# Sixteen more one-column matmuls at the head of TensorE's program, and half the columns on zeros behind the first scores, in a fused attention and feed-forward kernel

## The chip, the core and the metric

The kernel runs on one core of a Trainium2 chip. The core has four engines that compute: TensorE (PE for its matmuls, PEld for the loads of their stationary operands), VectorE (DVE), ScalarE (ACT) and GpSimd (POOL). SyncE (SP) issues the transfers, which sixteen DMA engines carry out. The metric is device time in microseconds, lower is better.

## What is computed

```python
# q, k, v: (8, 8, 576, 64); w_in (512, 2048), w_out (2048, 512)
scores = q @ k.T / sqrt(64)
# heads 0..3: local mask, 0 <= i - j < 32; heads 4..7: strided mask, i >= j and i % 32 == j % 32
attn = softmax(where(mask, scores, -1e9))
x = (attn @ v) laid out as (4608 tokens, 512 channels)
out = gelu(x @ w_in) @ w_out
```

## The kernel before, in words

The 4608 tokens are cut into 9 tiles of 512. Each tile goes through 16 pieces of the hidden layer: `ffn_h` sums a [128 x 512] block in 12 matmuls (lines 758 to 760: every operand is split into a rounded part and a rest, so each product takes three matmuls), `ffn_g` applies GELU on ScalarE and splits the result, and `ffn_o` adds the block's contribution to the output in another 12 matmuls (lines 796 to 798). The attention that feeds tile t + 1 is worked out beside the hidden layer of tile t: local heads with small matmuls on TensorE and a softmax on VectorE and ScalarE, strided heads almost wholly on VectorE.

The first tile has nothing to hide behind. Its local blocks are four jobs, L0 to L3 (`local_job`): scores by 8 matmuls of the program from the block's `qk` load (line 322), four masked score reductions on VectorE (line 280), four exponentials on ScalarE (line 285), sum and reciprocal (289, 292), a scaling (298, on VectorE for L0, L2 and L3), four transposes on TensorE (line 328), a copy (330), 8 matmuls with v (line 336), and the split of the result (305, 307). Its strided heads are two halves, `a0` and `b0` (`half_tile`: scores at line 455, mask and softmax at 464 to 478, transposes at 482, copy of the transposed weights into `va` at 484), which `strided_tile` (`A0`) joins: 32 matmuls of [32 x 32] per half at line 498 and transposes on VectorE at 503. The copy at 484 of the second half stands in the program behind the matmuls of the first half, and it reads a PSUM tile into which these matmuls write too.

The order of all this is written out by hand in the string `START`. Each word advances one job by a step (`L2` is the next step of block 2, `a0` the next of the first strided half), or issues a load: `q2 q0 q1 q3` are the loads of the four blocks' queries and keys (line 222), `S0` and `T0` those of the strided queries and keys (423), `v0` to `v3` the values (229), `w0`, `W0`, `w1` and on the weights (153), `B0` the strided values (441), `K1` the keys of the second tile (237). While the string is run, the order on all five engines is the string's. A word `z` and a digit is filler: one matmul on zeros into a spare PSUM tile (line 949), with 512 columns shifted right by the digit, so `z0` has 512, `z1` 256 and `z2` 128. In the main loop behind the string TensorE, VectorE and ScalarE stay in the order of the program; SyncE and GpSimd are ordered there by the framework's scheduler, which estimates when things happen.

Ahead of the string TensorE's program has a lead-in on zeros: one-column matmuls (line 897) and one matmul with 512 columns (line 898). A matmul with 32-bit floating-point operands is issued as two in the trace: the 48 of line 897 stand there as 96, each with its own load of weights; the small matmuls of the attention and the filler are doubled likewise. Those of the hidden layer, in another format, are not.

Of the kernel before, what the change touches and what calls it, by code (L numbers as in the profile page):

```python
# [47 lines left out]

NB = 16
START = """  # L50
    q2 q0 L2 z1 L0 L2 q1 S0 L0 L2 T0 L1 L2 L2 q3 L2 L1 v1 L2 L0 L0 v0 L1 v2 L0 L2 a0 w0 L0 a0 L1 a0 a0 b0 L3
    a0 b0 L1 b0 a0 b0 B0 L1 L3 b0 z0 L0 w1 L2 L3 b0 W0 a0 v3 a0 w2 b0 a0 b0 b0 K1 c0 L3 L2 L1 z2 a0 w3 L3 z2
    b0 L1 a0 L3 c0 z2 A0 W1 b0 A0 c1 c0 w6 w4 L2 c0 L0 L3 A0 L0 w5 L1 c1 A0 L1 w8 L3 A0 z0 c0 d0 e L0 L0 L3
    L3 L1 L3 w7 h0 E c1 f0 d0 w9 s1 c2 c2 d0 c1 f0 d0 c1 f1 c2 d0 V1 L4 f0 c3 d1 L5 d1 w10 f0 c3 w11 c2 c2
# [32 lines left out]
def attn_ffn_kernel(ctx: ExitStack, tc: tile.TileContext, qk, vl, qka, va, qs, ks, vs, s1, w, out):  # L87
# [732 lines left out]
    for u in range(U0, NU + 1):  # L820
# [12 lines left out]
        if av and qk_:  # L833
# [14 lines left out]
            i = next(i for i, x in enumerate(av) if x[1] == 0.6)  # L848
# [42 lines left out]
    def nil(p, n):  # L891
        return nc.const_aps.tensor(0.0, [p, n], F32)

    lead_in = ps_h.tile([P, TT], F32, name="lead_in", tag="H")
    for i in range(48):
        h = i % HL
        nc.tensor.matmul(lead_in[h * 32:h * 32 + 1, 0:1], nil(D, 1), nil(D, 1), start=True, stop=True, tile_position=(0, h * 32))
    nc.tensor.matmul(lead_in, nil(P, P), nil(P, TT), start=True, stop=True)
# [320 lines left out]
```

## Time and profile before

| what | value |
|---|---|
| three runs | 846.58, 848.91 and 2593.85 us |
| median | 848.91 us |
| profiled execution, own time | 848.29 us |
| its span, first to last instruction | 846.5 us (1.8 us lie outside it) |
| mean granted TensorE clock over the span | 0.996 of full speed |

Times in the views are microseconds from the start of the span. A row of the timeline has start, length, engine, line, operation, output and input with their shapes, and how many instructions were merged; in brackets the time for which the engine stood idle before them and what ended that, "issue" being a wait that nothing in the trace explains. A releaser is the event that came last before the wait ended, and can be another engine's that happened to finish then. Matmuls overlap, so the step from one start to the next is what one costs, and the length is more.

### The profile page before, as it was taken

To read this page: it belongs to the slowest core of one execution; us is meant where nothing else is said; L and a number is where in the kernel's file an instruction comes from. 1 tells how busy PE (TensorE), PEld (TensorE's weight loads), DVE (VectorE), ACT (ScalarE), POOL (GpSimd) and SP (SyncE) were. 2 spreads that over 40 slices of the span, in tenths; PEclk is the share of its full clock that TensorE was granted. 3 is DMA by queue.
4 is the path that set the end of the run, shared out by engine and by line. 5 is a ranking of instruction groups with operands and counts; after the bars stand their busy time and mean duration, and the time that the engine had idled before them with its cause. 6 is when DMAs were issued, how large, how long until landed. Compare 5 with 4: busy or idle time off the path is not lost.

```text
span 846.5 us, 15032 instructions
## 1 busy us (share of the span) xinstructions
PE 838.3 (99%) x5442; PEld 690.0 (82%) x5442; DVE 640.3 (76%) x1859; ACT 441.0 (52%) x862; POOL 18.1 (2%) x88
## 2 busy tenths in 40 slices
PE   8999999999999999999999999999999999999997
PEld 5788888888888888888888888888888888888886
DVE  6899989995999589958999698878887988521110
ACT  6898866552664355544553266545552456332222
POOL 5000000000000000000000000000000000000000
PEclk9899999999999999999999999999999999999999
DMA  9965241211220220223021222112102310100001
GB/s 342 416 256 194 64 144 52 68 37 64 99 63 14 92 101 9 69 60 136 7 63 35 78 86 69 42 63 100 60 13 93 101 38 13 36 34 17 1 0 50
DMA packets 27978, 69.40 MB, mean 82 GB/s; under 512 B 5888, under 2 KB 14208, under 8 KB 25856
## 3 DMA queue, kind: packets, MB, share of 16 engines
q1 hardware_dynamic: 27904, 68.44, 22.9%
q8 instruction: 43, 0.70, 0.3%
q14 instruction: 31, 0.25, 0.1%
HBM read 54.78 MB, written 9.44 MB: 76 GB/s over the span
## 4 chain that ended last, share of the span: by engine, by line
PE 98%; POOL 1%; DVE 1%; issue 0%; ACT 0%; POOLq 0%
PE H L758 16%; PE H L759 15%; PE H L760 15%; PE O L796 15%; PE O L798 15%; PE O L797 15%; PE S_x L404 2%; PE S L363 1%; PE S_L L336 0%; PE busy L949 0%; PE A L498 0%; PE S_L L328 0%; POOL bmask L913 0%; PE A L455 0%; POOL bmaskNone L913 0%
## 5 line engine op out<-in xcount | busy, mean ns | idle before, releaser
L798 PE MATMUL O<-w,gl 128*128 128x512 f32 x576 | 224.1, 389 | 0.0
L797 PE MATMUL O<-w,gh 128*128 128x512 f32 x576 | 224.1, 389 | 0.0
L796 PE MATMUL O<-w,gh 128*128 128x512 f32 x576 | 224.1, 389 | 0.0
L766 ACT ACTIVATE H<-H 128x512 f32<-128x512 f32 x144 | 83.8, 582 | 259.7 <-PE H L760 252.1
L770 DVE TENSOR_TENSOR gl<-H,gh 128x512 fp32r<-128x512 f32 x144 | 99.1, 688 | 157.4 <-ACT gh L768 157.3
L768 ACT CAST gh<-H 128x512 fp32r<-128x512 f32 x144 | 84.5, 587 | 118.2 <-PE O L797 113.7
L797 PEld LDWEIGHTS O<-w,gh 128*128 128x128 f32 x576 | 108.2, 188 | 22.6
L798 PEld LDWEIGHTS O<-w,gl 128*128 128x128 f32 x576 | 108.1, 188 | 22.4
L796 PEld LDWEIGHTS O<-w,gh 128*128 128x128 f32 x576 | 108.1, 188 | 22.4
L758 PE MATMUL H<-dh,w 128*128 128x512 f32 x288 | 114.3, 397 | 0.0
L759 PE MATMUL H<-dl,w 128*128 128x512 f32 x288 | 112.3, 390 | 0.0
L760 PE MATMUL H<-dh,w 128*128 128x512 f32 x288 | 112.2, 390 | 0.0
L759 PE MATMUL H<-xl,w 128*128 128x512 f32 x288 | 112.2, 390 | 0.0
L758 PE MATMUL H<-xh,w 128*128 128x512 f32 x288 | 112.2, 389 | 0.0
L760 PE MATMUL H<-xh,w 128*128 128x512 f32 x288 | 112.1, 389 | 0.0
L653 DVE TENSOR_TENSOR av<-sv,sc 128x320 f32<-128x320 f32 (+12 forms) x192 | 102.1, 564 | 6.8 <-DMA sv<-in_vs_dram 6.5
L601 DVE TENSOR_TENSOR qk<-sk,sq 128x320 f32<-128x320 f32 (+5 forms) x200 | 103.6, 545 | 0.0
L605 DVE TENSOR_REDUCE sc<-qk 128x5 f32<-128x320 f32 (+5 forms) x200 | 102.4, 538 | 0.0
L657 DVE TENSOR_REDUCE acc<-av 128x32 f32<-128x544 f32 (+16 forms) x192 | 101.2, 556 | 0.2
L766 ACT ACT_TABLE_LOAD x51 | 65.4, 1283 | 0.9
L758 PEld LDWEIGHTS H<-dh,w 128*128 128x128 f32 x288 | 54.2, 188 | 12.2
L760 PEld LDWEIGHTS H<-dh,w 128*128 128x128 f32 x288 | 54.1, 188 | 11.5
(123 smaller groups left out, 802.8 us busy)
## 6 DMA issues: line engine op xcount, KB each, us to landing
ws<-in_w_dram SPq DMA_DIRECT2D x14, 1023.8 KB, 9.9
qk<-in_qk_dram SPq DMA_DIRECT2D x8, 1280.0 KB, 5.6
vl<-in_vl_dram SPq DMA_DIRECT2D x8, 1024.0 KB, 4.8
out_dram<-ob SPq DMA_DIRECT2D x32, 256.0 KB, 2.3
sk<-in_ks_dram SPq DMA_DIRECT2D x8, 576.0 KB, 4.9
sv<-in_vs_dram SPq DMA_DIRECT2D x8, 576.0 KB, 3.8
band<-PT_L SPq DMA_DIRECT2D x224, 16.0 KB, 1.8
sq<-in_qs_dram SPq DMA_DIRECT2D x4, 448.0 KB, 3.6
```

What stands on the lines that cost most here:

```text
L601: nc.vector.tensor_tensor(tmp, sq[vi, "k"][:, c0:c1, :], sq[vi, "q"][:, r0 + r, :].unsqueeze(1).to_broadcast([P, n, D]), ALU.mult)
L605: nc.vector.tensor_reduce(ss[u][:, r, c0:c1], at[0], AX.X, ALU.add)
L653: nc.vector.tensor_tensor(tmp, sq[vi, "v"][:, d0:d1, 0:wr], ss[u][:, r, 0:wr].unsqueeze(1).to_broadcast([P, n, wr]), ALU.mult)
L657: nc.vector.tensor_reduce(ss[u, "acc"][:, r, d0:d1], at[0], AX.X, ALU.add)
L758: last[0] = nc.tensor.matmul(hp, w1[f][:, 0, c, :], xh, start=(i == 0), stop=False)
L759: last[0] = nc.tensor.matmul(hp, w1[f][:, 0, c, :], xl, start=False, stop=False)
L760: last[0] = nc.tensor.matmul(hp, w1[f][:, 1, c, :], xh, start=False, stop=(i == NC - 1))
L766: gelu[n] = nc.scalar.activation(hp, hp, AF.Gelu)
L770: nc.vector.tensor_tensor(gl, hp, gh.bitcast(F32), ALU.subtract)
L796: last[0] = nc.tensor.matmul(o, gh[:, sl], w2[f][:, 0, :], start=(f == 0), stop=False)
L797: last[0] = nc.tensor.matmul(o, gh[:, sl], w2[f][:, 1, :], start=False, stop=False)
L798: last[0] = nc.tensor.matmul(o, gl[:, sl], w2[f][:, 0, :], start=False, stop=(f == NF - 1))
```

## The change

The word `z1` behind the first step of L2 becomes `z2`: that filler has 128 columns instead of 256. The loop of one-column matmuls runs 64 times instead of 48. Nothing else is edited.

```diff
 START = """
-    q2 q0 L2 z1 L0 L2 q1 S0 L0 L2 T0 L1 L2 L2 q3 L2 L1 v1 L2 L0 L0 v0 L1 v2 L0 L2 a0 w0 L0 a0 L1 a0 a0 b0 L3
+    q2 q0 L2 z2 L0 L2 q1 S0 L0 L2 T0 L1 L2 L2 q3 L2 L1 v1 L2 L0 L0 v0 L1 v2 L0 L2 a0 w0 L0 a0 L1 a0 a0 b0 L3
...
     lead_in = ps_h.tile([P, TT], F32, name="lead_in", tag="H")
-    for i in range(48):
+    for i in range(64):
         h = i % HL
         nc.tensor.matmul(lead_in[h * 32:h * 32 + 1, 0:1], nil(D, 1), nil(D, 1), start=True, stop=True, tile_position=(0, h * 32))
     nc.tensor.matmul(lead_in, nil(P, P), nil(P, TT), start=True, stop=True)
```

## Rows read from the trace of the kernel before

**Rows 1.** The profile's page: the chain of work that ended last, shares of the span by engine.

```profile
PE 98%; POOL 1%; DVE 1%; issue 0%; ACT 0%; POOLq 0%
```

**Rows 2.** Busy time by stretches (from and to, length, then for each engine its busy time and in brackets its instructions, the granted clock of TensorE, the DMA engines' busy share and GB/s).

```profile
0.00:20.10 20.10, 16.34 (x390) 11.82 (x394) 12.23 (x65) 13.45 (x48) 11.92 (x54) 1.00 0.90 338
20.30:26.90 6.60, 6.60 (x64) 4.37 (x56) 4.79 (x11) 4.04 (x10) 0.00 (x0) 0.50 1.01 420
...
100.00:842.00 742.00, 742.00 (x4550) 613.42 (x4548) 552.99 (x1541) 356.99 (x700) 5.95 (x32) 1.00 0.17 57
```

**Rows 3.** Timeline of TensorE's matmuls from the start to the first transposes.

```profile
0.77 0.91 PE L897 MATMUL lead_in<-const-float32-0.0 64*1 64x1 f32 x96 [0.77 <-PEq L1206]
1.61 2.07 PE L898 MATMUL lead_in<-const-float32-0.0 128*128 128x512 f32 x2
3.70 1.54 PE L322 MATMUL S_L<-qk 64*64 64x96 f32 x16
5.18 1.22 PE L949 MATMUL busy<-const-float32-0.0 128*128 128x256 f32 x2
6.33 1.62 PE L322 MATMUL S_L<-qk 64*64 64x96 f32 x32
9.24 0.28 PE L328 MATMUL S_L<-ident,early 128*96 128x128 f32 x1 [1.29 <-POOL bmask L913]
```

**Rows 4.** Timeline of VectorE and, last line, of ScalarE between the scores of L2 and its first transpose (rows between them left out).

```profile
5.30 0.26 DVE L280 CUSTOM_DVE_ANT_0 early<-S_L,pbig 128x96 f32<-128x96 f32 x1 [0.68 <-PE S_L L322]
...
7.34 0.26 DVE L280 CUSTOM_DVE_ANT_0 pbig<-S_L,pbig 128x96 f32<-128x96 f32 x1 [1.24 <-PE S_L L322]
...
8.05 0.17 DVE L289 TENSOR_SCALAR ss_L<-ss_L 128x4 f32<-128x4 f32 x1
...
8.47 0.62 DVE L298 TENSOR_TENSOR early<-early,rs_L 128x384 f32<-128x384 f32 x1
...
6.96 0.19 ACT L285 ACTIVATION_READ_ACCUMULATOR early<-early,nm_L 128x1 f32 x1
```

**Rows 5.** DMA issues between 1.14 and 1.30 us: the one load `q0`, issued at 1.18 us (output and input, queue, count, KB, us from issue to landing).

```profile
qk<-in_qk_dram SPq DMA_DIRECT2D x1, 320.0 KB, 4.7
```

**Rows 6.** Timeline of TensorE from the first half of the matmuls at line 498 to the second filler, and VectorE's copy that stands between the halves (last line).

```profile
16.79 0.94 PE L498 MATMUL A<-va 32*32 32x64 f32 x64
18.21 0.34 PE L498 MATMUL A<-va 32*32 32x64 f32 x17 [0.48 <-DVE va L484]
19.68 0.79 PE L498 MATMUL A<-va 32*32 32x64 f32 x47 [1.13 <-issue]
20.40 1.09 PE L328 MATMUL S_L<-ident,early 128*96 128x128 f32 x4
21.42 1.98 PE L336 MATMUL S_L<-pbig,vl 96*64 96x64 f32 x32
23.33 2.08 PE L949 MATMUL busy<-const-float32-0.0 128*128 128x512 f32 x2
...
17.73 0.42 DVE L484 COPY va<-A 128x256 f32<-128x256 f32 x1 [0.53 <-PE A L498]
```

**Rows 7.** The page's DMA queue that carries instructions in large packets (packets, MB, share), and the page's line of busy times and instruction counts.

```profile
q8 instruction: 43, 0.70, 0.3%
...
PE 838.3 (99%) x5442; PEld 690.0 (82%) x5442; DVE 640.3 (76%) x1859; ACT 441.0 (52%) x862; POOL 18.1 (2%) x88
```

**Rows 8.** The same queue's line in four short windows, 3.1 to 3.3, 16.9 to 17.1, 23.3 to 23.5 and 31.4 to 31.6 us: in each of them one packet begins, the first four of the span.

```profile
q8 instruction: 1, 0.02, 30.2%
...
q8 instruction: 1, 0.02, 38.9%
...
q8 instruction: 1, 0.02, 30.8%
...
q8 instruction: 1, 0.02, 33.5%
```

**Rows 9.** Timeline of TensorE around the scores of the second tile (line 363) and just before; the twelve matmuls of a hidden block stand on each side of it.

```profile
25.33 1.12 PE L336 MATMUL S_L<-PT_L,vl 96*64 96x64 f32 x16
26.39 0.78 PE L758 MATMUL H<-dh,w 128*128 128x512 f32 x1
26.98 0.42 PE L759 MATMUL H<-dl,w 128*128 128x512 f32 x1
...
29.62 1.48 PE L363 MATMUL S<-qk 64*32 64x64 f32 x128
31.04 0.50 PE L758 MATMUL H<-dh,w 128*128 128x512 f32 x1
```

**Rows 10.** Timeline of TensorE between 9.7 and 14.7 us; from 12.58 on the same kinds of work as in the stretch of the lower clock. From 12.58 up to 16.79 the view has 36 matmuls.

```profile
9.78 2.06 PE L455 MATMUL A<-qka 128*64 128x32 f32 x64
11.77 0.88 PE L322 MATMUL S_L<-qk 64*64 64x96 f32 x16
12.58 1.13 PE L949 MATMUL busy<-const-float32-0.0 128*128 128x512 f32 x2
13.54 0.60 PE L328 MATMUL S_L<-ident,pbig 128*96 128x128 f32 x4
14.07 0.69 PE L336 MATMUL S_L<-PT_L,vl 96*64 96x64 f32 x16
14.69 0.64 PE L328 MATMUL S_L<-ident,pbig 128*96 128x128 f32 x4
```

## The prediction

> **What bounds the kernel now.** I read the page first: the chain that ended last is 98% TensorE [rows 1]. The stretches then show where that holds. From 20.3 us on TensorE is busy in every microsecond, 742.0 of 742.0 us between 100 and 842 [rows 2]; nothing there is touched by the change, so whatever the head gains or loses by about 20 us moves the end by the same amount, and nothing that follows can give it back. In the first 20.1 us it is busy for 16.34 only. [...] A measurement of this kernel can tell about 2% from no change, 17 us. The change cannot reach that by any mechanism that I find in the trace; what follows is about where in the last percent it lands.
>
> **The lead-in.** The 96 one-column matmuls in the trace start at 0.77 and the next line starts at 1.61: 0.84 us, 8.75 ns each. Sixteen more in the program are 32 in the trace, 0.28 us. The 512-column matmul behind them ends as L2's scores start, at 3.70 [rows 3], so those move to 3.98. VectorE's reductions of L2 move from 5.30 to 5.58, and ScalarE's last read for L2 from 6.96 to 7.24. VectorE needs that only at 8.05, for line 289 [rows 4]: hidden, with 0.6 us of slack.
>
> **The filler.** From 5.18 to 6.33 is 1.15 us for 256 columns; 512 took 2.09 [rows 3]. Halving the 1.15 gives 0.58, taking off the 0.47 that 128 columns cost by the difference gives 0.68. I take 0.6, the filler being most like itself. It then runs from 5.46 to 6.06, and L0's scores start at 6.06 instead of 6.33. Their load is there: q0 is issued at 1.18 and lands 4.7 us later, 5.9 [rows 5], which also bounds the gain at 0.45. This start is on the path: VectorE waits 1.24 us for it, reduces L0 from 7.34, and only then does lines 289, 292 and 298 for L2, which end at 9.09 and release the transposes at 9.24 [rows 3, 4]. (The releaser printed there is GpSimd's mask, which the transposes don't read; VectorE's scaling, which they do, ended 0.15 us before.) Sixteen matmuls of L2 took 1.54 us, 32 of L0 and L1 1.62 [rows 3]: the clock's level doubled near the start of these 32. So the 0.27 us won are run at half speed and worth about 0.14 at L0's end. **Term one: -0.14 us** at 9.24, between 0 and -0.45.
>
> **The moved block boundary.** The 1.13 us behind 18.55 stand inside one loop of small matmuls, 17 done and 47 to go, with operands already in use: no data can be missing there, and the view says "issue" [rows 6]. One DMA queue carries instructions: 43 packets, 0.70 MB, 16 KB each [rows 7]. TensorE alone has enough for it: 10,884 matmuls and loads over 43 packets are 253 a packet. One packet begins near 17.0 us, and TensorE goes on at 19.68 [rows 8, 6]. I read this as the next block of TensorE's program that came 1.13 us late, 2.7 us after its packet began, with the DMA engines full (share 0.90 up to here [rows 2]).
>
> The change puts 32 matmuls and 32 loads ahead, so the block ends 32 matmuls sooner in the old stream: 17 of these lie in the second half of line 498 and 15 in the first. That is a worse place. The 15 must run (15 of 64 at 0.94 us: 0.22), then VectorE's copy at line 484 can start (0.48 from 17.73 to 18.21), and then the whole second half must run, 0.94 [rows 6]. So if the block arrives at R, the transposes that started at 20.40 start at R + 1.64. With R still at 19.68 that is 21.32, 0.92 later. But the block before it is entered sooner too; if that is what asks for the next one, the request moves. 128 matmuls back from the late boundary (17 + 64, the 36 ahead of them and 11 more) is the fifth of the 16 scores at 11.77, about 12.0 us; 32 further back is the 37th of the 64 strided scores, about 10.9 [rows 6, 10]. With term one that is 1.24 us sooner, R is 18.44, and the transposes start at 20.08, 0.3 sooner. Which it is depends on where the request falls in queues that hold several microseconds of data, and the trace does not show it; I take the middle. **Term two, with term one in it: +0.3 us**, from -0.3 to +0.9. Without any wait for the block the transposes would start at 20.40 - 1.13 - 0.14 = 19.1, so -1.3 is the lower end.
>
> The next boundaries move as well. Behind the late one stand 47 + 4 + 32 + 2 + 16 + 12 = 113 matmuls up to line 363 [rows 6, 9], so by about 128 to a block the next boundary is now 15 matmuls into line 363 (29.7 us) and the following one 15 behind its end (34 us). Both go 32 sooner: to the end of line 336 (25.9) and to 17 before the end of line 363 (30.85). Between two boundaries there are then 5.0 us instead of 4.4, but the packets now begin 1.8 us (31.5) or 3.7 us (23.4) behind the boundary [rows 8] and need 2.7 more: 25.9 + 1.8 + 2.7 = 30.4 to 25.9 + 3.7 + 2.7 = 32.3, against 30.85. **Term three: +0.2 us**, from 0 to +1.4; I take it near the lower end, since the last packet measured, with fewer loads in flight, is the nearer one.
>
> [...]
>
> **Sum.** 0.3 + 0.2 = 0.5 on the profiled execution's own 848.29 us: 848.8. That execution lies 0.6 below the median of the runs shown, 848.91, of which the lowest is 846.58; so 848.8 also says "the same as the median".
>
> **The rivals.**
>
> *Both blocks late (slower).* The requests do not move in time, only the places where they are needed. Then term two is at its upper end, +0.9, and term three at +1.4: 850.6. It decides from R above 18.8 and a third packet that begins later than 2.2 us behind its boundary. For it: the packet began near 17.0 after loads that were issued long before, so a request 1 us sooner may stand in the same place. Against: packet delays differ a good deal, 1.8 and 3.7 us.
>
> *The boundary costs nothing.* The wait at 18.55 has another cause, stays with its matmuls or goes; the sum is term one, or at best -1.3: 847.0 to 848.15, say 848.1. For it: only one such wait is in the trace. Against: nothing else that is late ends at 19.68.
>
> *The clock does not fall at 20.2.* The waits before 20.2 lie elsewhere, and TensorE keeps the upper level. The price is in rows at both levels: four transposes 1.02 against 0.53 us, 32 matmuls with v 1.91 against twice 0.62, the filler 2.00 against 0.96, 16 more 1.06 against 0.62, the first matmul of the hidden block 0.59 against the 0.24 of its others [rows 6, 9, 10]. That is 0.49 + 0.67 + 1.04 + 0.44 + 0.35 = 3.0 us: 845.3. For it: the fall came behind waits of 0.48 and 1.13 us that the change moves. Against: it does not remove them.
>
> *The clock rises later than 6.5.* Half the filler is gone in front of the rise. L0's matmuls then run at the lower level throughout, eight steps of the program at 0.19 instead of 0.10 (+0.2 on before, after the sooner start), the transposes cost 0.49 more and the first strided scores, 32 of the 64 in 2 us, about 1.0 more: +1.7, 850.0. For it: 0.55 us less filler against 0.28 us more one-column matmuls, which fill little of the array. Against: TensorE is hardly ever idle there, before or after. [...]
>
> **How the numbers follow.** The forecast has 0.45, both blocks late 0.20, the clock that does not fall 0.13, the boundary that costs nothing 0.12, the later rise 0.08. Another 0.02 is for what no row shows: the scheduler's order of transfers in the main loop may come out otherwise, which would need to cost 17 us to count. Range: from 845.3, the whole price of the lower clock given back, to 851.0, both blocks late and 0.4 for the spread of single runs. That leaves out the cases in which two of the slower ones come together. Faster by over 2%: 0.01; within 2%: 0.97; slower by over 2%: 0.02.
>
> **What would show it.** Right: 128 matmuls at line 897, L0's scores near 6.06, the transposes near 9.10; a wait named "issue" inside the first half of line 498, with the copy at 484 behind it; the stretch at 0.50 still some 6.6 us long. Wrong: the wait stays behind 17 matmuls of the second half, or is gone; a wait of over 0.5 us inside line 363; L0's scores held by their load; TensorE idle anywhere behind 35 us; or a time outside 832 to 866.

## The result and the profile after

The changed kernel takes 852.38 us (851.77 to 852.69), the kernel before, run beside it, 847.49 us. The ratio is 1.0059, with a 95% interval of 1.0042 to 1.0075: slower by 4.9 us, inside the 2% that count as no change, outside the forecast's range (845.3 to 851.0). The two profiled executions, 848.29 and 851.77 us, are 3.48 apart; that difference can be followed through their traces. Of 83 further runs of the kernel before (one of 1044.88 us left out), 60 have a mean granted clock of 0.998 or more and a median of 847.0 us, the other 23 a lower clock and a median of 848.5. The profiled execution of the kernel before, at 0.996, is of the rarer kind and lies 0.8 us over the median, the changed kernel's 0.6 under its own; that makes up the other 1.4 us.

TensorE's timeline of the kernel after, columns as in [rows 3]; left out are rows that the text does not use:

```profile
0.77 1.17 PE L897 MATMUL lead_in<-const-float32-0.0 64*1 64x1 f32 x128 [0.77 <-PEq L1206]
1.87 2.07 PE L898 MATMUL lead_in<-const-float32-0.0 128*128 128x512 f32 x2
3.87 1.55 PE L322 MATMUL S_L<-qk 64*64 64x96 f32 x16
5.35 0.79 PE L949 MATMUL busy<-const-float32-0.0 128*128 128x128 f32 x2
6.07 1.86 PE L322 MATMUL S_L<-qk 64*64 64x96 f32 x32
8.96 0.61 PE L328 MATMUL S_L<-ident,early 128*96 128x128 f32 x4 [1.03 <-ACT pbig L285]
...
16.71 0.95 PE L498 MATMUL A<-va 32*32 32x64 f32 x64
18.14 0.85 PE L498 MATMUL A<-va 32*32 32x64 f32 x64 [0.48 <-DVE va L484]
18.93 0.64 PE L328 MATMUL S_L<-ident,early 128*96 128x128 f32 x4
...
22.53 1.15 PE L336 MATMUL S_L<-PT_L,vl 96*64 96x64 f32 x16 [0.82 <-ACT PT_L L330]
...
26.55 1.31 PE L363 MATMUL S<-qk 64*32 64x64 f32 x109
31.84 0.64 PE L363 MATMUL S<-qk 64*32 64x64 f32 x19 [3.97 <-issue]
32.41 0.80 PE L758 MATMUL H<-dh,w 128*128 128x512 f32 x1
33.00 0.63 PE L759 MATMUL H<-dl,w 128*128 128x512 f32 x1
...
37.43 0.40 PE L796 MATMUL O<-w,gh 128*128 128x512 f32 x1
```

Beside [rows 3, 6, 9] three things are to be seen. The first block wait, 1.13 us inside line 498, is gone: the second half runs through, and the transposes behind it start at 18.93 instead of 20.40. Line 363 is reached at 26.55 instead of 29.62. And behind 109 of its 128 matmuls stands a wait of 3.97 us, again "issue".

The stretches of the kernel after, columns as in [rows 2]:

```profile
18.90:26.50 7.60, 6.64 (x75) 4.61 (x66) 7.56 (x19) 7.17 (x15) 0.00 (x0) 1.00 1.02 421
26.50:30.20 3.70, 1.37 (x110) 1.17 (x110) 2.26 (x3) 3.64 (x5) 0.00 (x0) 1.00 1.01 412
30.30:37.00 6.70, 5.16 (x30) 4.02 (x30) 4.28 (x20) 2.28 (x4) 0.00 (x0) 0.50 1.01 412
37.20:100.00 62.80, 62.80 (x278) 51.99 (x277) 58.10 (x210) 55.35 (x92) 0.24 (x2) 1.00 0.54 205
```

The lower clock (0.50) no longer begins at 20.2 us but at 30.3, within the long wait. Under it the 12 hidden matmuls behind line 363 take 5.02 us (32.41 to 37.43), against 2.89 before (31.04 to 33.93). The account of the 3.5 us: -3.07 up to line 363 (1.47 of it by the transposes, which start at 18.93 and not 20.40, and 1.60 from there on, 7.62 against 9.22 us, at the upper clock but with a wait of 0.82 us for ScalarE's copy); +4.44 from there to the next hidden block (5.86 against 1.42 us), of which 3.97 are the wait; +2.13 for those 12 matmuls. Sum +3.50, and the spans differ by 850.0 - 846.5 = 3.5. From 37.2 us on TensorE is busy throughout (745.5 of 745.5 us between 100 and 845.5), and the matmuls keep this distance to those of the kernel before to the end (3.50 us at the first output block, 3.45 at the last matmul): nothing gave it back.

The instruction queue of the kernel after, as in [rows 8], in four windows of 0.2 us from 4.3, 13.3, 20.6 and 29.3 us:

```profile
q8 instruction: 1, 0.02, 29.6%
...
q8 instruction: 1, 0.02, 33.6%
...
q8 instruction: 1, 0.02, 32.1%
...
q8 instruction: 1, 0.02, 33.5%
```

The second packet begins near 13.4 instead of 17.0 us, so its block is there in time. The fourth begins near 29.4, when TensorE has stood for 1.5 us, and TensorE goes on 2.4 us later.

### The profile page after: what moved, and what is told of

The parts are those of the page before. It is cut to its first block, busy times and chain, and to the rows that moved or that the text cites. A ratio compares the mean times of both kernels' runs of the same rounds, so it can differ in the third digit from the quotient of the medians.

```text
span 850.0 us, 15096 instructions
## 1 busy us (share of the span) xinstructions
PE 838.1 (99%) x5474; PEld 690.5 (81%) x5474; DVE 640.5 (75%) x1859; ACT 440.9 (52%) x862; POOL 17.9 (2%) x88
## 4 chain that ended last, share of the span: by engine, by line
PE 96%; DMA 2%; ACT 1%; issue 1%; SPq 0%
PE H L758 16%; PE H L760 15%; PE H L759 15%; PE O L797 15%; PE O L798 15%; PE O L796 15%; PE S_x L404 2%; PE S L363 1%; DMA ws<-in_w_dram 1%; DMA qka<-in_qka_dram 1%; ACT dh L506 0%; SPq L222 0%; PE S_L L336 0%; ACT lead L174 0%; ACT ob L803 0%
```

## The experiments

The theory: TensorE's program comes in blocks of 256 instructions (128 matmuls and their loads; the waits below stand 256 apart, within one); 32 more matmuls at the head move every block end 32 matmuls sooner in the stream; what counts is where an end falls and how long its packet stands behind data. A packet here is the transfer of 16 KB that brings one block; I take it to be asked for when TensorE enters the block before. Rivals: the shorter filler, the number of one-column matmuls as such, an operand of line 363. Fences show the profiled execution; the intervals are those of all compared runs.

**One half of the change each.** `e1_lead64_z1` and `e2_lead48_z2`.

```diff
 # e1: the kernel before, with        # e2: the kernel before, with
-    for i in range(48):               -    q2 q0 L2 z1 L0 ...
+    for i in range(64):               +    q2 q0 L2 z2 L0 ...
```

> 64 one-column matmuls at the head, the filler left at 256 columns. Theory (the 32 extra matmuls in the trace move the ends of TensorE's program blocks, and one of them now ends inside line 363): as the changed kernel, 852 us, with a wait named issue of 3 to 5 us behind 109 of the 128 matmuls of line 363, the wait at 18.55 gone, the lower clock behind the long wait. Rival (half the filler makes the difference, by the clock or by L0's start): as the kernel before, 847.5 us, the wait of 1.1 us behind 17 matmuls of line 498's second half.

> 48 one-column matmuls, the filler at 128 columns. Theory (block ends): no block end moves, so as the kernel before, 846.5 to 848.5 us, the wait behind 17 matmuls of line 498's second half stays, none inside line 363, L0's scores 0.3 us sooner. Rival (filler): 852 us.

The lead-in alone gives 851.92 us, ratio 1.0046 (1.0033 to 1.0059); the filler alone 847.72, ratio 1.0003 (0.9992 to 1.0013). The filler is out. In e2 the first wait stands where it stood:

```profile
18.42 0.34 PE L498 MATMUL A<-va 32*32 32x64 f32 x17 [0.48 <-DVE va L484]
19.95 0.71 PE L498 MATMUL A<-va 32*32 32x64 f32 x47 [1.18 <-issue]
```

Of e1's twelve runs ten took 851.1 to 853.2 us and two 847.2 and 847.7; the profile is one of these two. It missed the expected wait, and shows how the wait can stay away. Its strided values landed late:

```profile
17.77 0.84 PE L498 MATMUL A<-va 32*32 32x64 f32 x64 [0.87 <-DMA va<-in_va_dram]
...
29.22 1.48 PE L363 MATMUL S<-qk 64*32 64x64 f32 x128
30.63 0.50 PE L758 MATMUL H<-dh,w 128*128 128x512 f32 x1
```

and the stretch from 20.3 to 26.9 was at the lower level:

```profile
20.30:26.90 6.60, 6.60 (x56) 4.32 (x55) 5.47 (x14) 5.18 (x12) 0.00 (x0) 0.50 1.01 415
```

TensorE came to the block end 2.6 us later than in the changed kernel, at about 30.4, the packet had begun near 27.9, and there was no wait. The packet itself was sooner, too: its request falls near 25.1, later than the 23.2 of the changed kernel, and it still began 1.6 us before that kernel's. A slower head goes with 4 us saved; the ten runs near 852 have no trace.

**Other places of the block ends.** `e8_lead56_z2` (56 one-column matmuls), `e12_lead32_z2` (32) and `e3_lead112_z2` (112: a whole block more than 48), all with the shorter filler.

```diff
-    for i in range(64):
+    for i in range(56):    # e12: 32, e3: 112
```

> 56 one-column matmuls: block ends 16 matmuls sooner than before. They should fall behind 1 matmul of line 498's second half and behind 125 of line 363's 128. Theory: if the first wait is gone, TensorE reaches line 363 near 26.6 us and waits there 3 to 5 us behind 125 matmuls: 851 to 853 us; if the first wait stays, no wait at line 363 and 847 to 848.5 us. Rival (the cost grows with the number of one-column matmuls): half of 5 us, 850 us, without a wait at these places.

> 32 one-column matmuls: block ends 32 matmuls later than before, behind 49 matmuls of line 498's second half and 47 of line 363's 128, and 47 behind line 363's end. Theory: a wait of 0.3 to 1.5 us behind 49 of line 498's second half or none, none inside line 363 (its block was asked for at 19 us), 846.5 to 849 us, whichever the clock does. Rival (the fewer one-column matmuls the better, by 5 us for 16): 843 us.

> 112 one-column matmuls: 256 matmuls and loads more in the trace than the kernel before, one whole block of 16 KB. Theory (block ends): the blocks end at the same matmuls as in the kernel before, so the wait is back behind 17 matmuls of line 498's second half or near it, there is none inside line 363, and the time is that of the kernel before plus at most 0.6 us of lead-in, 847 to 848.5 us. Rival (each one-column matmul more costs, by delaying everything or by its own): 16 cost 5 us, so 64 cost 5 us or more, 852 us and up.

With 56 the time is 852.3 us, ratio 1.0056 (1.0043 to 1.0068), and the wait stands behind 125 of line 363, as counted:

```profile
26.79 1.44 PE L363 MATMUL S<-qk 64*32 64x64 f32 x125 [0.19 <-DMA qk<-in_qk_dram]
32.96 0.42 PE L363 MATMUL S<-qk 64*32 64x64 f32 x3 [4.72 <-issue]
```

In both the changed kernel and this one the clock fell within the wait; the stretch here:

```profile
30.60:37.20 6.60, 4.24 (x12) 3.30 (x12) 3.80 (x20) 2.13 (x3) 0.00 (x0) 0.50 1.00 410
```

With 32 it is 848.17, ratio 1.0006 (0.9995 to 1.0017), and the only such wait stands behind 49 of line 498, as counted; behind it the clock did not fall (last line):

```profile
19.22 0.72 PE L498 MATMUL A<-va 32*32 32x64 f32 x49 [0.48 <-DVE va L484]
21.04 0.34 PE L498 MATMUL A<-va 32*32 32x64 f32 x15 [1.11 <-issue]
...
20.00:30.00 10.00, 8.43 (x211) 6.26 (x212) 9.00 (x20) 8.28 (x15) 0.00 (x0) 1.00 1.01 415
```

With 112 it is 849.81, ratio 1.0030 (1.0019 to 1.0040): neither the 847 to 848.5 of my theory nor the 852 of the rival. I had overlooked that the block more also has an end more, and that it falls into the lead-in itself, before anything hides it:

```profile
0.78 1.96 PE L897 MATMUL lead_in<-const-float32-0.0 64*1 64x1 f32 x223 [0.78 <-PEq L1206]
6.61 0.16 PE L897 MATMUL lead_in<-const-float32-0.0 64*1 64x1 f32 x1 [3.88 <-issue]
...
22.72 0.85 PE L498 MATMUL A<-va 32*32 32x64 f32 x64 [0.48 <-DVE va L484]
...
30.58 1.48 PE L363 MATMUL S<-qk 64*32 64x64 f32 x128
```

The wait expected in line 498 did not come, none stood in line 363, as expected. Counted in instructions that TensorE has begun (matmuls, loads and the few others of its program in the trace), the waits stand at 449 (e3), 706 (before, e2, e12), 962 (e4, below) and 1217 (after, e8): 256 apart, within one. That shows what the wait is, and that it depends on the place of the end, not on the number of one-column matmuls: 32, 48, 56, 64 and 112 give 848.2, 847.7, 852.3, 852.4 and 849.8.

**Ends moved behind the head only.** `e4_lead48_z2_16later`.

```diff
+        elif kind == "m":   # x one-column matmuls into the spare tile
+            ...
-    ... L3 A0 z0 c0 d0 e ...
+    ... L3 A0 z0 m16 c0 d0 e ...      # and 48 at the head, z2
```

> 48 one-column matmuls at the head, and 16 more behind the last filler of 512 columns (near 24 us), so that only block ends behind them move. Theory (block ends): the wait behind 17 matmuls of line 498's second half is there as before, with the lower clock behind it, and a second wait stands inside line 363 at 109 of 128; as TensorE comes there 3 us later than in the changed kernel, it is 0.5 to 3 us: 848.5 to 851 us. Rival (what the extra matmuls do happens at the head): as before, 847.5 us, no wait in line 363.

849.34 us, ratio 1.0023 (1.0014 to 1.0032), in the range, but in the profile not by the waits I expected. The one in line 498 was absent, and one stood at the end in between, inside line 336:

```profile
22.55 0.56 PE L336 MATMUL S_L<-PT_L,vl 96*64 96x64 f32 x10 [0.33 <-ACT PT_L L330]
24.21 0.45 PE L336 MATMUL S_L<-PT_L,vl 96*64 96x64 f32 x6 [1.10 <-issue]
...
29.11 1.48 PE L363 MATMUL S<-qk 64*32 64x64 f32 x128
```

That profile, 847.82 us, is the fastest of its runs, so it does not show what the others paid for.

**Less data in front of the packet.** `e5_after_loads_held`, and `e7_before_loads_held` with the same edit of the kernel before.

```diff
-    ... K1 c0 L3 ... w3 ... W1 ... w6 w4 ... w5 ... w8 ... e ... w7 h0 E c1 f0 d0 w9 s1
+    ... K1 c0 L3 ... h0 c1 f0 d0 p0 w3 W1 w6 w4 w5 w8 e w7 E w9 s1
 # p0: the next load waits for TensorE's latest matmul
```

> The changed kernel, with the ten loads behind K1 (w3, W1, w6, w4, w5, w8, e, w7, E, w9) issued only when the first hidden block's matmuls are done, so that the DMA engines have nothing but K1 queued when the block that line 363 needs is asked for near 23 us. Theory (the block of instructions stands behind data in its DMA engine's queue): its packet begins by 26 us instead of 29.4, the wait inside line 363 is 1 us or less, TensorE's clock does not fall at 30 us, and the time is 844.5 to 847 us, unless a weight is late. Rival (a block takes its 6 to 9 us from one packet to the next whatever the data do): packet at 29, wait of 4 us, 852 us.

> The kernel before with the same ten loads held, as the control of that edit. Theory: the first wait (1.1 us behind 17 matmuls of line 498's second half) and the lower clock behind it stay, since the loads queued at 12 to 17 us are the same, and nothing later waits for a block, before or after: 846.5 to 848.5 us, more only if weights come late. Rival (holding the loads is what helps by itself): 845 us.

In e5 the packet for line 363 begins between 26.7 and 26.9 us, 2.7 sooner than in the changed kernel:

```profile
q8 instruction: 1, 0.02, 43.0%
```

and the wait is 1.00 us; line numbers are one lower here:

```profile
27.07 1.32 PE L362 MATMUL S<-qk 64*32 64x64 f32 x109
29.39 0.41 PE L362 MATMUL S<-qk 64*32 64x64 f32 x19 [1.00 <-issue]
...
40.10 0.50 PE L796 MATMUL O<-w,gh 128*128 128x512 f32 x1 [1.17 <-DVE w L188]
```

The clock stays at the upper level behind it in this profile (1.00 from 27 to 40 us), the lowest of its six runs. So the shorter wait goes with the loads that were held (though e1's packet, with nothing held, also began only 2.8 us behind its block end), but data in front are not the whole delay:

```profile
25.00:26.70 1.70, 1.70 (x9) 1.41 (x8) 1.70 (x5) 1.67 (x3) 0.00 (x0) 1.00 0.00 0
```

From 25.2 us until the packet began, the DMA engines carried nothing at all; of the 3.0 us from the block end at 23.74 to the packet, data can explain at most the first 1.5. The time is 851.22 all the same (ratio 1.0049, 1.0037 to 1.0061), not 847: 1.3 us ahead of the kernel before at the first output block, it then waits for the weights that were held. The control is slower too, 850.77 (1.0046, 1.0030 to 1.0062; 848.5 was the most expected), with the same waits for weights near 40 us, and with a wait that I took for one of these:

```profile
30.84 0.39 PE L795 MATMUL O<-w,gh 128*128 128x512 f32 x1
32.96 0.50 PE L796 MATMUL O<-w,gh 128*128 128x512 f32 x1 [1.73 <-DVE w L188]
```

It stands at 1217 begun instructions, a block end, and that block's packet began at 30.55, 2.4 us before TensorE went on; the write of VectorE that the row names had ended at 32.53. So it is most likely a block again, this time among large matmuls. Against my expectation the wait in line 498 was absent in this trace and the clock did not fall (mean 0.999, the kernel before 0.996); TensorE was 3.1 us ahead of the kernel before at 31 us and lost it there and to the weights.

**Line 363 later, and a milder hold.** `e6_after_s1_later` and `e11_after_s1_L4_later` put line 363 behind the second hidden block; `e9_after_held_but_W1` and `e10_before_held_but_W1` hold the loads but for W1, the weight that e5 waited for.

```diff
 # e6: s1 behind f1; L4 behind the next f0      # e9, e10:
-  w9 s1 c2 ... f1 c2 d0 V1 L4 f0 c3 d1 L5       -  K1 c0 ... w3 ... W1 ... w9 s1
+  w9 c2 ... f1 s1 c2 d0 V1 f0 L4 c3 d1 L5       +  K1 W1 c0 ... h0 p0 w3 w6 w4 w5 w8 e w7 E w9 c1 f0 d0 s1
 # e11: L4 and L5 behind f0's fourth step
```

> The changed kernel, with the scores of the second tile (line 363) moved behind the second hidden block's 12 matmuls (and VectorE's reductions of them behind that block's GELU), so that the block end inside line 363 comes some 3 us later. Theory (the wait is a race between the packet at 29.4 and TensorE's arrival): the wait in line 363 shrinks from 4.0 to 0 to 1.5 us and the clock falls less or not, 845 to 849 us. Rival (the wait belongs to line 363's operands or its bank): it moves with line 363 and stays 4 us, 852 us.

> The changed kernel, line 363 behind the second hidden block's matmuls as in the run before, and VectorE's reductions of its scores behind the rest of the first GELU, for which TensorE waited 1.45 us there. Theory: the wait inside line 363 stays near 1.5 us, the other goes, the clock does not fall: 848 to 849.5 us. Rival (the reductions are then late for something else): 850.5 us or more.

> The changed kernel, nine loads held as in the run before (now from the middle of the first hidden block), but W1, the half weight for which TensorE waited 1.4 us at 38 to 40, issued right behind K1. Theory: the packet for line 363 begins by 27 us, the wait there is 0 to 1.2 us, no lower clock after 6.5, no wait for the second output block, and with the changed kernel's head 3 us ahead the time is 844.5 to 847 us, below the kernel before. Rival (late weights take back whatever is won): 849 us or more.

> The kernel before with the same edit of the loads. Theory: its late block in line 498 stays or goes with the state of the queue near 12 to 17 us, which the edit hardly touches; the next blocks come sooner: 845 to 848.5 us. Rival: 849 us or more, from late weights.

e6: 850.69 (ratio 1.0031, 1.0018 to 1.0044), over the 849 expected. The wait shrinks to 1.56 us, and the output block waits for VectorE:

```profile
32.88 0.46 PE L362 MATMUL S<-qk 64*32 64x64 f32 x31 [1.56 <-issue]
...
35.45 0.50 PE L797 MATMUL O<-w,gl 128*128 128x512 f32 x1 [1.45 <-DVE gl L769]
```

The 12 hidden matmuls that now stand ahead of line 363 move the wait from behind 109 of its matmuls to behind 97 (31 are left, not 19): it keeps its place in the count of instructions, not its operand. TensorE arrived 3.4 us later and waited 2.4 less. e11 takes the second wait away and keeps the first, 1.60 us: 849.34 (1.0020, 1.0011 to 1.0029), as expected. e9 comes to 850.92 (1.0030, 1.0015 to 1.0045; 847 at most expected) and e10 to 848.91 (1.0015, 1.0003 to 1.0026; 848.5 at most). e10's trace, 846.80 us, has no wait in line 498 and one of 0.92 us at the same matmul as the control's (32.55, packet at 30.20; the write that its row names had ended at 31.86). e9's runs spread from 846.8 to 852.3; its profile, 847.55 us, has no wait in line 363, but one of 1.10 us for the strided values and one of 0.87 for a weight, and what its slower runs waited for was not seen. No version is faster than the kernel before; the nearest, 48 or 32 one-column matmuls with the shorter filler, cannot be told from it.

## Why the prediction was wrong

The forecast was 848.8, within 2% with 0.97. The latter held; time and range did not. Step by step:

The forecast opens with the premise that what the head gains by 20 us moves the end, and that nothing behind can give it back. It failed: the head was 1.47 us ahead at 18.93 and 3.07 at line 363, and all of it was given back there, at a block end that the edit had moved.

The lead-in and the filler were right in kind. 128 matmuls stand at line 897, in 1.10 us; L0's scores start at 6.07 (6.06 forecast); the transposes at 8.96, 0.28 sooner (0.14 forecast). e2 shows that the filler alone moves nothing that can be measured.

The reading of the 1.13 us as a late block of instructions was right, and so were the places to which the ends move: "17 before the end of line 363" was 19. Not every end that TensorE crosses shows a wait (the kernel before has none at 29.7 us), but three stand 3.97, 3.88 and 4.72 us in the open, each behind small matmuls with the DMA engines busy (share 1.01, 0.84 in e3, 1.00 in e8).

**Term two** failed in sign. It had the transposes between 20.1 and 21.3; they started at 18.93, beyond even the case without any wait (19.1). I let the block come sooner only by as much as it is asked for sooner, 1.24 us at most; its packet moved by 3.6, from 17.0 to 13.4. A packet's delay is no constant that shifts along. With that the rival I gave 0.13, the clock that does not fall at 20.2, came true. That 3.07 us were won by line 363, as the 3.0 of that rival, is luck: 1.47 of them came before the transposes, and the upper clock gave 1.60, since TensorE then waited 0.82 for ScalarE.

**Term three** is the step that decides, and it was mis-sized: 0.2, at most 1.4, against 3.97 us of wait and 2.13 for the lower clock behind it. Two errors are in it. I took the delays of two packets, 1.8 and 3.7 us from boundary to packet, as ends of the range; here, from about 23.2 to 29.4, it was over 6. My own numbers had a third that I left out, from 12.0 to 17.0, 5 us, which would have put the wait at 2.8 us. And I set TensorE's arrival at 30.85 while another rival of mine had it 3 us sooner. I priced the rivals one at a time, 845.3 for the clock that stays, 850.6 for the blocks that come late, but they are coupled: the head that gains 3 us is the one that runs ahead of its instructions. The request for this block moved from 29.7 us in the kernel before to 23.2, by 6.5, its packet from 31.5 to 29.4, by 2.1. So the earlier arrival was paid back in full, and with more, since the clock fell as well. e1's trace, a late head without this wait at 847.7 us, fits this; its runs near 852 were not traced.

That the wait takes the clock was in no rival, though the trace of before had the pattern: waits, then 6.6 us at 0.50. In the changed kernel it is 0.50 from 30.3 to 37.0, from within the 3.97 us of wait on, and the 12 hidden matmuls there took 5.02 us against 2.89; behind e5's 1.00 us it is 1.00 throughout (27 to 40 us). The short waits do not sort that way: the clock fell behind before's 1.13 us and e2's 1.18, not behind e12's 1.11 (1.00 from 20 to 30 us) or e6's 1.56 (mean 0.999), and in e1 it fell at 20.2 without a wait for a block, behind 0.87 us for data and 0.48 for a copy. So the long wait's price is seen in two traces, the changed kernel's and e8's; what decides behind a short one stays open.

## What to carry to other kernels

The block ends kept their places in the count of begun instructions (waits at 449, 706, 962 and 1217), whatever stood ahead; so count what an edit adds, and compare the time that TensorE takes from one end to the next with the time that a block takes to come. In the changed kernel these were 4.4 us (23.2 to 27.7) and 8.6 us (23.2 to 31.8); a run of small matmuls makes the first short (109 of line 363 took 1.3). An end inside line 363 by itself cost nothing (the kernel before has one at 29.7 us, e12 one at 28.7), and one among large matmuls is not safe (waits of 1.73 us in e7, 0.92 in e10). Where two predicted effects meet in a race, as a faster head and a block that comes at its own time, work out their joint outcome, not each by itself. And look for the second price of a wait on TensorE: the clock behind it, here 2.13 us more for 12 matmuls behind 3.97 us of wait.

## What the runs showed of the hardware that I had not expected

From the beginning of a block's packet to TensorE's going on it took 2.4 to 2.7 us (17.0 to 19.68 before, 29.4 to 31.84 after, 26.8 to 29.39 in e5), with full DMA engines and, in e5, with engines that had carried nothing from 25.2 us until the packet (share 0.91 from 27 to 40 us); the traces show only the packet of it. From the boundary to the packet it took from 1.8 us (29.7 to 31.5 before) to 6.2 (23.2 to 29.4 after) while the DMA engines were full (share 0.99 and 1.01), and 3.0 in e5, where they stood idle for its last 1.6. Moving the request by about 1 us (12.0 to 11.0) moved the packet by 3.6; what sets its turn was not found.
